# Attention values taken two or three query blocks at a time in the early part of a fused attention and MLP kernel

## The chip, the cores and the metric

The kernel runs on one core of one Trainium2 chip. The metric is device time of one execution in microseconds (us). All matrix work is in 32-bit floating point. The engines are named as in the profile: PE (matrix products; PEld is its weight loading), DVE (vector), ACT (activation and copies), POOL (general elementwise) and SP (issues transfers).

## The reference

```python
# q, k, v: (8, 8, 576, 64); tau = 0.02; w_in: (512, 2048); w_out: (2048, 512)
scores = matmul(q, k^T) / 8
scores = where(scores >= max(scores) - tau, scores, -1e9)
attn   = exp(scores - max(scores));  attn = attn / (sum(attn) + 1e-9)
o      = matmul(attn, v)                       # (8, 8, 576, 64)
x      = o.transpose(0, 2, 1, 3).reshape(4608, 512)
out    = square(maximum(x @ w_in, 0)) @ w_out  # (4608, 512)
```

## The kernel before

Attention and the MLP run together as one stream on PE. Attention is cut into *visits* (one pair of heads of one batch, or half of it) and *steps* (one block of 128 queries of a visit; block 4 holds the last 64 queries of both heads of the pair). Steps are numbered s0, s1, and so on, in order of time:

- Visits 0 to 3 hold blocks 0 and 1 of the four head pairs of the first batch: steps s0 to s7.
- Visits 4 to 7 hold blocks 2, 3 and 4 of the same pairs: s8 to s19.
- Visits 8, 9 and 10 hold all five blocks of a pair of the second batch: s20 to s34.
- From visit 11 on (s35 and later) the weights are turned by DVE and placed by DMA ("by_dma"). The change does not touch these visits.

In a step, in this order: `scores` (L246) multiplies a block of queries by the keys into the PSUM tiles `s0` and `s1` (one for each head of the pair, one buffer each); DVE takes the row maximum (L268); ACT makes threshold and bias (L281, L282) and the exponents (L284); DVE applies the threshold and sums (L296), which also frees the PSUM tiles for the next step's scores; POOL divides (L304, L306). So each step's scores wait for the DVE threshold of the step before.

Two steps later `turn` turns the weights of the block on PE against the identity (L330, for block 4 L336 and L342), in three parts, each with an ACT copy into `wT` (L331, L338, L343). Parts 0 and 1 stand right behind the scores in PE's order, part 2 later in the step. `mix` (L432) multiplies the turned weights by the values `vs` into a PSUM bank, and `put` copies the result on ACT into `xT`, the input of the MLP (L415; the wide copies of the later visits have lines L419 and L426). In visits 0 to 10, before the change, there is one mix for each block, three steps after its scores: 128 columns wide, 64 for block 4. In PE's order it stands between the turn parts 1 and 2, with a quarter of the step's fill ahead of it. Turn parts 0, 1, 2 and the mix take PSUM banks 4 and 5 by turns (while `early()`, that is before s10, part 1 takes bank 6 or 7). One table says when a mix is made, `mixes`, and `complete` says from which step the tokens of an MLP chunk (256 tokens) may be used.

Between these parts PE is *filled* with MLP work, in pieces of some 1.8 us (`fill`, a quarter of the step's amount at each of four places): `mlp_in` (L480, with ACT L490 and POOL L491 behind it) and `mlp_out` (L519) for chunk 0, and seven `product`s (L552) for each later chunk. How many pieces a step gets is counted when the program is written, from constants, by `rate`: until step `out_from` (s34) only the 32 pieces of chunk 0 are spread, from s10 on.

In the same steps the MLP weights are loaded and rounded, 32 pieces in all, one in most steps from s8 to s34 and two in s15, s18 and s22. A piece takes two ACT instructions (L138, L139), two on DVE (L141, L143) and two on POOL (L145, L147), in this order. The second piece of a step has its ACT part behind the exponents and its DVE L141 ahead of the threshold L296. The `mlp_in` pieces of chunk 0 wait for the rounded `w_in_sb` (L147).

The order on every engine is the order in which the program is written; there is no scheduler behind it.

Of the kernel before, what the change touches and what calls it, by code (L numbers as in the profile page):

```python
# [19 lines left out]
def kernel(  # L20
# [10 lines left out]
    nc = tc.nc  # L31
    B, H, S, D = q.shape
    d_model, d_ff = moe_w_in.shape
    n_tokens = out.shape[0]
    P = 128
    HP = H // 2
    NPAIR = B * HP
    NBLK = S // P
    REST = S - NBLK * P
# [32 lines left out]
    wT = const.tile([P, NC9, S + REST], FP32, name="wT")  # L72
# [3 lines left out]
    at = RAW * 2 * WP  # L76
# [115 lines left out]
    def arrived(t):  # L192
        assert all(x[0].tensor.name != t.tensor.name for x in loads)
# [117 lines left out]
    def take(what, among):  # L311
        used[what] += 1
        return bank[among[used[what] % len(among)]]

    def next_bank():

        among = (4, 5, 6, 7) if state["step"] > first_dma + 2 else (6, 7)
        used["bank"] = min([x for x in among if x > used["bank"]] or among)
        return bank[used["bank"]]

    def turn(vis, i, part):

        w = weights[vis, i][0]
        ps = take("mm", (6, 7)) if early() and part == 1 else take("tx", (4, 5))
        ps = ps.rearrange("p (c n) -> p c n", n=P)
        if i < NBLK:
            cols = slice(i * P, (i + 1) * P)
            for n in range(3):
                c = 3 * part + n
                nc.tensor.transpose(ps[:, n, :], w.rearrange("p u k -> p (u k)")[:, c * P:(c + 1) * P], ident)  # L330
            nc.scalar.copy(wT[:, 3 * part:3 * part + 3, cols], ps[:, 0:3, :])  # L331
        elif part < 2:
            rows = slice(part * D, (part + 1) * D)
            for c in range(NBLK):
                at = part * REST + c * P
                nc.tensor.transpose(ps[:, c, 0:D], w[rows, 0, at:at + P], ident[rows, rows])  # L336
            at = part * (NBLK + 1)
            nc.scalar.copy(wT[:, at:at + NBLK, NBLK * P:S], ps[:, :, 0:D])  # L338
        else:

            for rows, keys in ((slice(0, D), slice(S - REST, S)), (slice(D, P), slice(0, REST))):
                nc.tensor.matmul(ps[rows, 0, 0:D], w[rows, 0, keys], ident[rows, rows], start=True, stop=True)  # L342
            nc.scalar.copy(wT[:, NBLK, NBLK * P:S], ps[:, 0, 0:D])  # L343

    blocks = {}

# [53 lines left out]
    def put(n, first, ps, by_32s):  # L400

        b, pr = divmod(visits[n][0], HP)
        count = ps.shape[1]
        lo = (b * S + first) % RING
        assert b * S + first + count - RING <= read_to["x"]

        def to(x0, x1):
            at = (lo + x0) % RING
            return xT[:, pr, at:at + x1 - x0]

        fit = min(RING - lo, count)
        if not by_32s:
            for x0, x1 in ((0, fit), (fit, count)):
                if x0 < x1:
                    nc.scalar.copy(to(x0, x1), ps[:, x0:x1])  # L415
            return
        src = ps.rearrange("p (b u q) -> p b u q", u=2, b=4)
        if fit == count:
            nc.scalar.copy(to(0, count).rearrange("p (u b q) -> p b u q", u=2, b=4), src)  # L419
            return  # L420

        for u in range(2):
            b0 = min(max((fit - u * P) // 32, 0), 4)
            for x0, x1 in ((0, b0), (b0, 4)):
                if x0 < x1:
                    nc.scalar.copy(to(u * P + x0 * 32, u * P + x1 * 32).rearrange("p (b q) -> p b q", q=32),  # L426
                                   src[:, x0:x1, u, :])

    def mix(n, cols):

        def term(ps, u, c, at, rows=slice(0, P), first=False, last=False):
            nc.tensor.matmul(ps[u * D:(u + 1) * D, :], vs[n % 2][rows, u * (NBLK + 1) + c, :],  # L432
                             wT[rows, NBLK if c == NBLK else u * (NBLK + 1) + c, at:at + ps.shape[1]],
                             start=first, stop=last)

        above, below = slice(0, D), slice(D, P)
        arrived(vs[n % 2])
        if not by_dma(n):
            ps = take("tx", (4, 5))[:, 0:cols.stop - cols.start]
            for c in range(NBLK):  # L440
                for u in range(2):
                    term(ps, u, c, cols.start, first=(c == 0))
            for u, rows in enumerate((above, below)):
                term(ps, u, NBLK, cols.start, rows, last=True)
            put(n, cols.start, ps, False)
            return
        n1, n2 = 2 * P + REST, 2 * P
        at = ODD if paired(n) and n % 2 else ONE
        one, two = (next_bank() for x in range(2))
        groups = (one[:, 0:n1], at, (above, below)), (two[:, 0:n2], TWO, (below, above))  # L450
        for c in range(NBLK):
            for ps, x, _ in groups:
                for u in range(2):
                    term(ps, u, c, x, first=(c == 0))

        for ps, x, places in groups:
            for u, rows in enumerate(places):
                term(ps, u, NBLK, x, rows, last=True)
        put(n, 0, one[:, ONE - at:ONE - at + 2 * P], True)
        left = ODD if at == ODD else LEFT - at  # L460
        put(n, NBLK * P, one[:, left:left + REST], False)
        put(n, 2 * P, two[:, 0:n2], True)
# [123 lines left out]
    FIRST = TCH // P  # L586
    visits = [(g_, list(range(FIRST))) for g_ in range(HP)] + [(g_, list(range(FIRST, NBLK + 1))) for g_ in range(HP)]
    visits += [(g_, list(range(NBLK + 1))) for g_ in range(HP, NPAIR)]

    def paired(n):  # L590

        return n >= 3 * HP
# [8 lines left out]
    def by_dma(n):  # L601

        return n >= 3 * HP - 1
# [6 lines left out]
    for s, (n, i) in enumerate(steps):  # L610

        if by_dma(n):
            mixed = {visits[n][1][-1]: (0, 4)}
        else:
            mixed = {x: (x, 3) for x in range(NBLK + 1)}
        if i in mixed:
            first, lag = mixed[i]
            cols = slice(first * P, S if by_dma(n) else min((i + 1) * P, S))
            mixes[s + lag] = (n, cols)
            g_ = visits[n][0]  # L620
            if g_ % HP == HP - 1:
                complete[s + lag] = g_ // HP * S + cols.stop
# [12 lines left out]
    def early():  # L635
        return state["step"] < min(chunk_at)
# [52 lines left out]
    for s, (n, i) in enumerate(steps):  # L689
        if s < HP * FIRST:  # L690
            x = int(n > 0 and i == 0)
        else:
            x = 2 if (n, i) in ((2 * HP - 2, FIRST + 1), (2 * HP - 1, FIRST + 1), (2 * HP, FIRST)) else 1
# [14 lines left out]
    for s, (n, i) in enumerate(steps):  # L708
# [20 lines left out]
        if more:  # L729
            a, b, c, d = (s + 1, s + 5, s + 7, s + 8) if paired(n) else (s + 1, s + 2, s + 4, s + 4)  # L730
# [26 lines left out]
    for s in range(END + 1):  # L757
# [9 lines left out]
        if on:  # L767
            n, i = steps[s]
            at = visits[n][1].index(i)
            last = at == len(visits[n][1]) - 1  # L770
# [15 lines left out]
        if old:  # L786
            turn(*old, 0)
            turn(*old, 1)
# [11 lines left out]
        if s in mixes and not old:  # L800
            mix(*mixes[s])
            for j in chunk_at.get(s, ()):
                add_chunk(j)
        quarter = rate(s) / 4 if s < END else 1e9
        fill(quarter)
        if s in mixes and old:
            mix(*mixes[s])
            for j in chunk_at.get(s, ()):
                add_chunk(j)
        if old:  # L810
            turn(*old, 2)
# [18 lines left out]
        if 0 < s <= NST and by_dma(steps[s - 1][0]):  # L830
            m, x = steps[s - 1]
# [54 lines left out]
```

## Time and profile before

| | |
|---|---|
| median of 3 runs | 1389.96 us (1389.86 to 1391.53) |
| the profiled execution's own time | 1391.53 us |
| its span, first to last instruction | 1389.8 us |
| PE / DVE / ACT / POOL busy, share of the span | 97% / 60% / 32% / 65% |
| mean granted PE clock | 0.995 of full |
| PE busy from 24.0 to 62.8 us (s3 to s9) | 34.59 of 38.80 us |
| PE busy from 62.8 to 146.9 us (s10 to s22) | 76.43 of 84.10 us |
| PE busy from 146.9 to 216.0 us (s23 to s34) | 66.40 of 69.10 us |
| PE busy from 249.0 to 1389.0 us | 1132.04 of 1140.00 us |

The profiled execution is the slowest of the three, 1.57 us above the median. A busy PE is PE with a matmul in flight. In the timeline a row merges instructions of one kind that follow each other; a bracket at its end gives the idle time of its engine ahead of it, and what ended it. A product in 32-bit floating point appears as two rows in the counts of the trace, so a mix of 10 products has x20.

### The profile page before, as it was taken

Reading aid. Unit: us, or ns where it says so; the run is one execution under the profiler, and the core shown is the slowest. Engines: PE = TensorE matmul, PEld = TensorE weight load, DVE = VectorE, ACT = ScalarE, POOL = GpSimd, SP = SyncE. Lnnn points to the kernel's source line nnn. Section 1 sums busy time; section 2 is a strip of 40 time slices with the busy share of each in tenths; the row PEclk is TensorE's granted clock in tenths of the full one; section 3 lists DMA queues with packets and bytes.
Section 4 is the critical chain, followed back from the end, with each engine's and each line's share of the span. In section 5 each row is a group of like instructions: output and inputs, shape, how many; then the busy total and the mean of one; then the engine's idle time right before and its main releaser. Section 6 shows DMA issues by size and latency. Waiting matters only on the chain.

```text
span 1389.8 us, 22678 instructions
## 1 busy us (share of the span) xinstructions
PE 1354.5 (97%) x7576; PEld 1039.6 (75%) x7576; DVE 828.9 (60%) x1866; ACT 439.8 (32%) x1068; POOL 899.3 (65%) x1211
## 2 busy tenths in 40 slices
PE   6898999999999999999999999999999999999998
PEld 5676556777777777787777778777777877788887
DVE  5877675967767676757565757566666665401001
ACT  4776674223232323232223232322222222210110
POOL 3678875668786968686767677676867655422332
PEclk8999999999999999999999999999999999999999
DMA  8763531445545455554445355544445544310000
GB/s 154 157 152 107 143 93 29 88 85 106 115 98 115 97 109 114 105 112 94 92 87 113 76 111 107 112 87 97 93 93 91 118 89 102 64 31 16 0 16 16
DMA packets 407748, 127.95 MB, mean 92 GB/s; under 512 B 390832, under 2 KB 396752, under 8 KB 407632
## 3 DMA queue, kind: packets, MB, share of 16 engines
q1 hardware_dynamic: 385344, 94.57, 36.1%
q0 software_dynamic: 19984, 31.63, 8.4%
q8 instruction: 61, 1.00, 0.3%
q10 hardware_dynamic: 2304, 0.29, 0.2%
q14 instruction: 55, 0.45, 0.1%
HBM read 50.59 MB, written 9.44 MB: 43 GB/s over the span
## 4 chain that ended last, share of the span: by engine, by line
PE 89%; DVE 3%; ACT 3%; POOL 2%; issue 1%; DMA 1%; SPq 0%; DVEq 0%; ACTq 0%; POOLq 0%
PE bank L480 34%; PE bank L552 29%; PE s L246 12%; PE bank L432 11%; PE bank L519 2%; PE bank L330 2%; ACT wT L331 1%; ACT w L284 1%; DVE wo L507 1%; DVE w L296 1%; DVE st L268 1%; POOL g L491 0%; POOL w L306 0%; POOL w_in_sb L147 0%; DVE wo L296 0%
## 5 line engine op out<-in xcount | busy, mean ns | idle before, releaser
L480 PE MATMUL bank<-xT,w_in_sb 128*128 128x256 f32 x2304 | 520.4, 382 | 3.2 <-POOL w_in_sb L147 2.1
L480 PEld LDWEIGHTS bank<-xT,w_in_sb 128*128 128x128 f32 x2304 | 430.8, 190 | 85.8 <-issue 22.2
L268 DVE TENSOR_REDUCE st<-s 128x1 f32<-128x576 f32 x286 | 204.1, 753 | 224.4 <-PE s L246 224.3
L296 DVE SCALAR_TENSOR_TENSOR w<-s,st,w 128x576 f32<-128x576 f32 x269 | 209.2, 815 | 120.6 <-ACT w L284 120.5
L552 PE MATMUL bank<-wo,gsum 128*128 128x256 f32 x1088 | 248.9, 382 | 2.4 <-POOL gsum L470 2.4
L306 POOL TENSOR_SCALAR w<-w,st 128x576 f32<-128x576 f32 x269 | 223.5, 840 | 25.2 <-DVE st L299 19.2
L552 PEld LDWEIGHTS bank<-wo,gsum 128*128 128x128 f32 x1088 | 203.9, 190 | 41.5 <-issue 9.8
L491 POOL TENSOR_TENSOR g<-g 128x512 f32<-128x512 f32 x144 | 152.1, 1057 | 96.4 <-ACT g L490 95.1
L281 ACT ACTIVATE st<-st 128x2 f32<-128x2 f32 (+1 forms) x148 | 30.3, 205 | 566.1 <-DVE st L268 565.4
L552 PE MATMUL bank<-wo,g 128*128 128x256 f32 x816 | 188.3, 382 | 0.0
L284 ACT ACTIVATE w<-s,st 128x576 f32<-128x576 f32 x269 | 183.3, 732 | 0.2 <-ACT st L282 0.2
L370 DVE STREAM_TRANSPOSE turned<-w 128x512 f32<-128x512 f32 (+2 forms) x388 | 168.8, 490 | 18.7 <-DMA wT<-turned 16.7
L246 PE MATMUL s<-kT,qT 64*128 64x288 f32 x1016 | 166.9, 435 | 12.1 <-DVE kT L226 4.9
L304 POOL TENSOR_SCALAR st<-st 128x2 f32<-128x2 f32 (+1 forms) x148 | 32.9, 222 | 221.6 <-DVE w L296 214.4
L552 PEld LDWEIGHTS bank<-wo,g 128*128 128x128 f32 x816 | 153.0, 190 | 30.0 <-issue 8.7
L432 PE MATMUL bank<-wT,vs 128*64 128x128 f32 (+7 forms) x1700 | 167.8, 356 | 5.1 <-ACT wT L331 3.5
L432 PEld LDWEIGHTS bank<-wT,vs 128*64 128x64 f32 (+1 forms) x1700 | 95.5, 136 | 76.8 <-issue 24.6
L490 ACT ACTIVATE g<-bank 128x512 f32<-128x512 f32 x144 | 86.1, 599 | 194.8 <-PE bank L480 194.2
L246 PEld LDWEIGHTS s<-kT,qT 64*128 64x128 f32 x1016 | 94.9, 189 | 69.1 <-issue 49.0
L190 POOL DMA_DIRECT2D vs<-in_v_dram x144 | 90.7, 635 | 0.0
L566 DVE TENSOR_TENSOR gsum<-g 128x512 f32<-128x512 f32 x34 | 23.0, 707 | 110.6 <-PE bank L552 110.6
L145 POOL TENSOR_TENSOR turned<-turned 128x512 f32<-128x512 f32 x32 | 41.1, 1288 | 40.7 <-DVE turned L143 34.9
(80 smaller groups left out, 1006.1 us busy)
## 6 DMA issues: line engine op xcount, KB each, us to landing
wT<-turned SPq DMA_DIRECT2D x800, 72.0 KB, 2.3
out_dram<-osb POOLq DMA_DIRECT2D x34, 256.0 KB, 2.8
wo<-in_moe_w_in_dram SPq DMA_DIRECT2D x16, 512.0 KB, 4.7
wo<-in_moe_w_out_dram SPq DMA_DIRECT2D x16, 512.0 KB, 3.6
ql<-in_q_dram POOLq DMA_DIRECT2D x96, 72.0 KB, 2.7
wT<-turned SPq DMA_DIRECT2D x192, 36.0 KB, 2.3
kl<-in_k_dram POOLq DMA_DIRECT2D x88, 72.0 KB, 3.0
vs<-in_v_dram POOLq DMA_DIRECT2D x48, 128.0 KB, 3.1
```

Source lines behind the costliest of these rows:

```text
L190: (nc.gpsimd if state["step"] > first_dma + 2 else nc.sync).dma_start(out=to, in_=src)
L246: nc.tensor.matmul(sc[u][to, half, 0:HALF], lhsT, keys[rows, half * HALF:(half + 1) * HALF], start=True, stop=True)
L268: nc.vector.tensor_reduce(out=mx[:, u:u + 1], in_=sc[u][:, :, 0:HALF], axis=AX.XY, op=ALU.max)
L284: nc.scalar.activation(out=w[:, u, :].rearrange("p (h k) -> p h k", h=2), in_=sc[u][:, :, 0:HALF], func=AF.Exp, bias=bias[:, u:u + 1], sca ...
L296: nc.vector.scalar_tensor_tensor(out=wu, in0=sc[u][:, :, 0:HALF], scalar=thr[:, u:u + 1], in1=wu, op0=ALU.is_ge, op1=ALU.mult, accum_out=s ...
L306: nc.gpsimd.tensor_scalar(out=w[:, u, :], in0=w[:, u, :], scalar1=z[:, u:u + 1], scalar2=rcp[:, u:u + 1], op0=ALU.add, op1=ALU.mult)
L370: nc.vector.transpose(wb[:, at:at + k1 - k0, i % 2, :], w[:, u, k0 * 32:k1 * 32].rearrange("p (k q) -> p k q", q=32))
L432: nc.tensor.matmul(ps[u * D:(u + 1) * D, :], vs[n % 2][rows, u * (NBLK + 1) + c, :], wT[rows, NBLK if c == NBLK else u * (NBLK + 1) + c, a ...
L480: nc.tensor.matmul(h[:, x % 2, :], w_in_sb[:, c, f * P:(f + 1) * P], xT[:, c, at:at + TCH], start=(c == 0), stop=(c == NMC - 1))
L490: nc.scalar.activation(out=to, in_=h, func=AF.Relu)
L491: nc.gpsimd.tensor_tensor(out=to, in0=to, in1=to, op=ALU.mult)
L552: nc.tensor.matmul(to, left[:, f, :], wo[:, slot, f, :], start=(f == 0), stop=(f == HF - 1))
```

## The change

Visits 0 to 10 are mixed in two goes instead of block by block: blocks 0 and 1 together (256 columns), three steps after block 1's scores, and blocks 2, 3 and 4 together (320 columns), three steps after block 4's scores. So 35 mixes (28 of 128 columns, 7 of 64) become 14 (7 of 256 columns, 7 of 320), with 10 products each as before, and 35 copies by `put` become 14. The mixes that stay keep their places in PE's order; 21 are gone: those of s3, s5, s7, s9, of s11, s12, s14, s15, s17, s18, s20, s21, and of s23, s25, s26, s28, s30, s31, s33, s35, s36.

Since the turned weights of a half visit now wait longer for their mix, half visits put theirs in two places of `wT` by turns (`column`): columns 0 to 319 for even visits, 320 to 639 for odd ones. Whole visits keep theirs.

```diff
+    def column(vis, i):
+
+        first = visits[vis][1][0]
+        return i * P if len(visits[vis][1]) > NBLK else vis % 2 * (S + REST) // 2 + (i - first) * P
+
     def turn(vis, i, part):
 ...
         if i < NBLK:
-            cols = slice(i * P, (i + 1) * P)
+            cols = slice(column(vis, i), column(vis, i) + P)
 ...
-            nc.scalar.copy(wT[:, at:at + NBLK, NBLK * P:S], ps[:, :, 0:D])
+            x = column(vis, i)
+            nc.scalar.copy(wT[:, at:at + NBLK, x:x + D], ps[:, :, 0:D])
 ...
-            nc.scalar.copy(wT[:, NBLK, NBLK * P:S], ps[:, 0, 0:D])
+            x = column(vis, i)
+            nc.scalar.copy(wT[:, NBLK, x:x + D], ps[:, 0, 0:D])
 ...
         if not by_dma(n):
             ps = take("tx", (4, 5))[:, 0:cols.stop - cols.start]
+            at = column(n, cols.start // P)
             for c in range(NBLK):
                 for u in range(2):
-                    term(ps, u, c, cols.start, first=(c == 0))
+                    term(ps, u, c, at, first=(c == 0))
             for u, rows in enumerate((above, below)):
-                term(ps, u, NBLK, cols.start, rows, last=True)
+                term(ps, u, NBLK, at, rows, last=True)
 ...
         if by_dma(n):
             mixed = {visits[n][1][-1]: (0, 4)}
         else:
-            mixed = {x: (x, 3) for x in range(NBLK + 1)}
+
+            mixed = {FIRST - 1: (0, 3), NBLK: (FIRST, 3)}
```

In the built program the instructions on DVE, POOL and SP stand in the same order as before, row by row. On PE and ACT the 21 mixes and their copies are missing and 14 are wider; nothing else has moved.

## The prediction

> **What bounds the kernel now.** First the page: busy shares, the span in slices and the PE clock.
>
> ```profile
> PE 1354.5 (97%) x7576; PEld 1039.6 (75%) x7576; DVE 828.9 (60%) x1866; ACT 439.8 (32%) x1068; POOL 899.3 (65%) x1211
> ...
> PE   6898999999999999999999999999999999999998
> ```
>
> PE is the bound, but not everywhere. From 249 us on it idles 8 of 1140 us, and the change leaves that part alone: whatever s3 to s37 gain or lose shifts it as a whole. The early part, 24 to 249 us, has idle PE: 4.2 us in s3 to s9, 7.7 in s10 to s22, 2.7 in s23 to s34. So I went through the timeline there step by step, asking of each step whether PE's work or something else lets the next scores start.
>
> A step before s10, in PE's timeline (s4, then the scores of s5):
>
> ```profile
> 33.57 1.46 PE L432 MATMUL bank<-wT,vs 128*64 128x128 f32 x20
> 34.96 0.55 PE L330 MATMUL bank<-ident,w 128*128 128x128 f32 x3
> 36.15 1.94 PE L246 MATMUL s<-kT,qT 64*128 64x288 f32 x8 [0.65 <-DVE wo L296]
> ```
>
> The mix takes 1.39 us (33.57 to 34.96); then PE waits 0.65 us for the threshold. The loop scores, maximum, exponents, threshold, scores sets these steps (5.26 us each), not PE. Later, with pieces of MLP work in the steps, PE sets most, but not all. All engines in s15, a step with two weight pieces:
>
> ```profile
> 95.72 1.35 ACT L284 ACTIVATE w<-s,st 128x576 f32<-128x576 f32 x2
> ...
> 96.96 0.66 ACT L138 ACTIVATE turned<-wo 128x512 f32<-128x512 f32 x1
> 97.72 0.43 DVE L141 TENSOR_SCALAR turned<-turned 128x512 uint32<-128x512 uint32 x1 [1.15 <-ACT turned L138]
> 98.06 0.81 DVE L296 SCALAR_TENSOR_TENSOR w<-s,st,w 128x576 f32<-128x576 f32 x1
> ...
> 99.03 1.21 PE L246 MATMUL s<-kT,qmid 128*128 128x288 f32 x4 [0.90 <-ACT wT L343]
> ```
>
> The second piece's L138 and L141 stand ahead of the threshold; PE starts 0.23 us after the first L296 has ended (98.80), whatever the bracket names. PE in s17:
>
> ```profile
> 107.68 0.70 PE L480 MATMUL bank<-xT,w_in_sb 128*128 128x256 f32 x2 [0.50 <-POOL w_in_sb L147]
> 108.91 0.70 PE L480 MATMUL bank<-xT,w_in_sb 128*128 128x256 f32 x2 [0.53 <-POOL w_in_sb L147]
> ```
>
> Here POOL's rounding is late; its chain hangs on s16, not on PE.
>
> **The price of a mix.** The narrow ones are in the trace: 1.39 us for 128 columns and, from the next rows, 0.88 (82.31 to 83.19) for 64.
>
> ```profile
> 82.31 0.95 PE L432 MATMUL bank<-wT,vs 128*64 128x64 f32 x20 [0.24 <-ACT wT L331]
> 83.19 0.55 PE L330 MATMUL bank<-ident,w 128*128 128x128 f32 x3
> ```
>
> The wide ones occur only in later visits, where one mix does a 256- and a 320-column group:
>
> ```profile
> 291.92 4.79 PE L432 MATMUL bank<-wT,vs 128*64 128x320 f32 x40
> 296.63 1.99 PE L480 MATMUL bank<-xT,w_in_sb 128*128 128x256 f32 x8
> ```
>
> 4.71 us over 576 columns, shared by columns: 2.10 for 256 and 2.62 for 320. The upper bound goes on from the narrow rows, 0.51 us for each 64 columns: 2.41 and 2.92. I take the lower, since those rows have the widths themselves. PE work before: 28 x 1.39 + 7 x 0.88 = 45.1 us; after: 7 x (2.10 + 2.62) = 33.0. Freed 12.1 us (7.8 by the upper bound). A step that loses its mix gives PE 1.39 us; one that keeps it pays 0.71 (256 for 128) or 1.74 (320 for 64).
>
> **Step by step.** Freed PE time counts only down to the time at which the threshold or POOL lets the next scores start; an added cost counts in full wherever PE has no idle time. Ready times are those at which L296 ends, plus the 0.22 us seen above.
>
> - s3 to s9: the removals free nothing (PE idles already; s3 ends on the threshold too, 30.66). The 256s in s4 and s8 put 0.71 against 0.65 idle, +0.09 each with rounding; s6 has 0.95 idle: 0. Sum +0.2.
> - s10, s11: s10 pays 0.71, has 0.33 idle. But s11's maximum starts at 69.43, behind L143 of DVE, not behind the scores, so s10's loss is absorbed and s11 gives a little: -0.15.
> - s12 (-1.39; two fill pieces, PE sets it) and s13 (+1.74): +0.35.
> - s14 -1.39. s15: nothing, the threshold sets it. s16 +1.74. s17 -1.39, and the two POOL waits of 0.50 and 0.53 go as well: L147 is ready at 107.6 and 108.85, while s16 has made PE 1.74 later. Sum -2.07.
> - s18: nothing (1.22 idle ahead of s19, second piece again). s19 +1.74, s20 -1.39 and two waits of 0.54 and 0.54, s21 -0.3 (threshold). Sum -1.0.
> - s22 to s24: POOL is behind by a step there (busy without a gap from 147.07 to 163.9), and L139, queued on ACT behind L147 and ahead of the turn copies, holds s24's mix until 155.24. Counted from the start of s22 (139.26): that mix still starts at +16.0, then 2.10 + 0.38 + two pieces of 3.53 give s25 at +22.06, against 21.28. The 1.39 of s23 is lost in that wait: +0.78.
> - s25 -0.8, s26 -0.3 (thresholds ready 165.06 and 170.93 against scores at 166.41 and 171.77; the second head's half comes 0.8 later and takes part of it), s27 +1.74: +0.64.
> - s28 -0.7 (threshold 183.46, scores 184.41), s29 +0.71: 0.
> - s30 -0.4, s31 -0.1, s32 and s33 together +0.82 (s33 falls to its loop, 4.55 from 5.66), s34 0.71 less 0.33 idle: +0.7.
> - s35 -1.36, s36 -1.39 (three pieces and more, PE sets them), s37 +1.74: -1.0.
>
> Sum -1.5 us. Of 12.1 us freed, over ten vanish: the mixes spread the work evenly, and in two goes the full steps grow fuller while the emptied ones hit the loop.
>
> Costed at nothing: `put`. 28 x 0.265 + 7 x 0.217 us of copies go, 7 x 0.383 and 7 x about 0.43 (between the 256-wide 0.383 and the 384-wide 0.482 of L331) come: ACT gains 3.2 us. The copies stand behind the exponents; queued behind them are the turn copy and the weight pieces, read a step later. If they were on the loop, that is 3.2 us more gain at most, and a loss of 0.2 at each 320. The turn part 2 now reuses the bank of part 0 and waits for its copy, as the removed mix did (0.24 us, kept in the times above). Chunk 1 joins the queue a step later (s22), when only chunk 0's pieces are dealt: 0. The values of visit 2 and 3 overwrite those of visit 0 and 1 after a mix that ends 0.71 later; SP's queue has q and k loads behind, but issues at 38.08 what s7 and s8 read: 0, or 0.7 once for each if SP had no slack.
>
> **The clock.** Windows of 2 us; columns: PE, PEld, DVE, ACT, POOL busy, then the clock:
>
> ```profile
> 14.00:16.00 2.00, 0.00 (x0) 0.00 (x0) 1.86 (x7) 1.72 (x5) 0.20 (x1) 0.99 0.79 205
> 16.00:18.00 2.00, 0.24 (x2) 0.27 (x4) 1.99 (x4) 0.85 (x2) 1.66 (x3) 0.50 1.01 389
> ...
> 26.00:28.00 2.00, 2.00 (x8) 1.24 (x7) 1.74 (x3) 0.17 (x1) 1.83 (x4) 0.50 0.73 118
> 28.00:30.00 2.00, 2.00 (x21) 1.50 (x19) 1.18 (x3) 1.84 (x6) 2.00 (x2) 0.59 0.94 203
> ```
>
> PE stops at 12.85, and at 16 the clock is halved; it comes back at about 29.6, after PE has run without a gap since 23.97. The mix of s3 lies in that run (28.36 to 30.35). Without it PE runs from 23.97 to about 28.95 and then idles until 30.86. If the clock then stays halved into s4, s4 costs: scores 3.0 for 1.9, turns 1.5 for 0.9, half the mix at half speed: together about +2.3 us. In s5, s7 and s9 PE now idles 1.4 + 0.65 = 2.0 us at a stretch; the largest idle stretch at which the clock stayed up is 0.95 (s6), the one that lost it was over 3. I take 2.0 as harmless, being nearer the first.
>
> [...]
>
> **The rivals.**
>
> *Little gain* (42%): the sum above, clock back in s3: 1389.96 - 1.5 = about 1388.5. The profiled execution is 1.57 us above the median; the difference is applied to the median. Its own range is 1386 to 1391.
>
> *Clock late once* (20%): -1.5 + 2.3: 1390.8. For it: the run of s3 is cut from over 10 us to 5. Against: 5 us is as long as PE needed before.
>
> *More of the freed time comes through* (20%): in s11, s21, s25, s26, s28, s30 and s31 the loop keeps back 7 x 1.39 - 2.75 = 7.0 us. Part of what sets it is DVE's L141, 0.42 us when alone but 1.0 to 1.5 in several of these steps while POOL works; with POOL further ahead after the long steps it may shrink. Half of the 7.0 gives -5: 1385; all of it -8.5: 1381.5.
>
> *Slower: the clock falls in the emptied early steps* (18%). If an idle stretch of 2.0 us is enough, each of s5, s7, s9 hands a halved clock to s6, s8, s10. The price of a halved clock is in s3: 6.92 us against 5.26 for the same work, 1.66, and up to 2.3 with a 256-column mix. With s4's that is about +8: 1396.5. It decides once idle stretches between 0.95 and 3.1 us are enough. The upper price of the wide mixes (+0.3 in ten steps set by PE) makes the same side, +1.5 net.
>
> That the change doesn't do what it says I exclude: in the built program 35 mixes are 14 wide ones.
>
> **How the numbers follow.** 1388.5 is the likeliest. The range holds little gain, late clock with the upper mix price (1390.8 + 3.0 = about 1394), and the third case to half and somewhat over (1383); left out are its far end and most of the slower one. A measurement of this kernel can tell about 0.2%, 2.8 us: below 1387.2 or above 1392.7. Faster: 20% from the third case and 13% from the first, whose step limits are each good to a few tenths. Slower: 18%, 5% from the second, 2% from the first. The same: 42%.
>
> **What would show it.** Right: scores still 5.26 us apart from s5 to s9 with 2 us of PE idle in s5, s7, s9; the POOL waits of s17 and s20 gone; s15 and s18 as long as before (6.34 and 6.66 us); wide mixes of 2.1 and 2.6 us; from s38 on the same spacing as before. Wrong: a PE clock under 1 after 33 us, steps without a mix shorter than 4.5 us with two heads, or a lasting difference after 250 us.

## The result, and the profile after

| | before | after |
|---|---|---|
| median | 1389.95 us (4 runs, 1389.86 to 1391.53) | 1399.72 us (4 runs, 1398.81 to 1400.27) |
| ratio | | 1.0067, 95% interval 1.0049 to 1.0084 |
| span of the profiled execution | 1389.8 us | 1398.5 us |
| mean granted PE clock in it | 0.995 | 0.984 |
| the same, 30 to 73 us | 1.00 | 0.74 |

The kernel became 0.7% slower, 9.8 us. The forecast was 1388.5 with a range of 1383 to 1394; the rival that had the clock falling in the emptied early steps, 1396.5, named the cause.

From the page of the changed kernel: the busy time and instruction count of each engine, the PE clock in 40 slices, and the group of `mlp_in` products (now L488).

```profile
PE 1357.4 (97%) x7156; PEld 1027.4 (73%) x7156; DVE 826.4 (59%) x1866; ACT 440.1 (31%) x1047; POOL 898.9 (64%) x1211
...
PEclk7799999999999999999999999999999999999999
...
L488 PE MATMUL bank<-xT,w_in_sb 128*128 128x256 f32 x2304 | 519.3, 382 | 1.1 <-ACT osb L533 1.1
```

PE has 420 rows fewer and yet 2.9 us more busy time: part of its work ran at half speed. The clock is down in the first two slices (0 to 70 us); before it was down in the first alone. (It also falls for 3.4 us each at 107.1 and 127.6 us, too short to show in a slice.) The POOL waits of `mlp_in` are gone, as forecast. Now the windows of 2 us, with columns as in the prediction (PE busy first, PE clock third from the end):

```profile
38.00:40.00 2.00, 1.79 (x15) 1.17 (x11) 1.32 (x2) 0.83 (x2) 1.83 (x3) 1.00 0.88 174
40.00:42.00 2.00, 0.00 (x0) 0.00 (x0) 2.00 (x4) 1.90 (x6) 2.00 (x3) 1.00 0.98 270
42.00:44.00 2.00, 1.69 (x6) 1.57 (x7) 1.22 (x6) 1.29 (x3) 0.79 (x3) 0.57 0.57 101
44.00:46.00 2.00, 2.00 (x9) 1.10 (x6) 1.40 (x2) 0.00 (x0) 1.12 (x2) 0.50 0.53 84
46.00:48.00 2.00, 2.00 (x10) 1.14 (x10) 0.43 (x2) 1.67 (x5) 0.00 (x0) 0.50 0.77 125
48.00:50.00 2.00, 2.00 (x14) 1.05 (x12) 1.71 (x5) 0.86 (x2) 0.00 (x0) 0.72 0.89 201
```

PE stands still from 39.79 to 42.31, in the emptied s5, and the clock is halved just as s6 begins. PE's timeline of the same stretch:

```profile
38.59 1.20 PE L335 MATMUL bank<-ident,w 128*128 128x128 f32 x9
42.31 2.99 PE L246 MATMUL s<-kT,qT 64*128 64x288 f32 x8 [2.52 <-DVE w L296]
45.23 1.54 PE L335 MATMUL bank<-ident,wo 128*128 128x128 f32 x6
46.70 3.70 PE L439 MATMUL bank<-wT,vs 128*64 128x256 f32 x20
50.33 0.55 PE L335 MATMUL bank<-ident,wo 128*128 128x128 f32 x3
```

Nine turns in a row (parts 0, 1, 2), then 2.52 us of nothing, then scores in 2.99, turns in 1.54 and the mix in 3.63 us (46.70 to 50.33). With the clock up, the same scores and turns took 1.94 and 0.87 us before (s6, 41.41 to 44.16), and a mix of this width takes 2.46 (first run below). The starts of the steps say what this costs, in us from one step's scores to the next one's:

| step | s4 | s5 | s6 | s7 | s8 | s9 | s10 | sum |
|---|---|---|---|---|---|---|---|---|
| before | 5.26 | 5.26 | 5.57 | 5.26 | 5.26 | 5.32 | 4.59 | 36.52 |
| after | 8.25 | 4.90 | 8.50 | 4.89 | 8.63 | 4.83 | 6.38 | 46.38 |

Those seven steps lose 9.9 us. In s6, s8 and s10 the clock had just fallen, at 42.28, 55.9 and 69.6 us. In s4 it had not come back yet: it was halved from 15.0 to 35.5 us, where before it was halved from 16.0 to 29.6. From s11 to s41 the two profiled executions part by 0.6 us more, and before s4 the one of before was 1.7 us later by its own start: 9.9 + 0.6 - 1.7 is the 8.7 by which the spans differ.

### The profile page after: what moved, and what is told of

Its sections match the earlier page's. It is cut to its first block, busy times and chain, and to the rows that moved or that the text cites. A ratio compares the mean times of both kernels' runs of the same rounds, so it can differ in the third digit from the quotient of the medians.

```text
span 1398.5 us, 21810 instructions
## 1 busy us (share of the span) xinstructions
PE 1357.4 (97%) x7156; PEld 1027.4 (73%) x7156; DVE 826.4 (59%) x1866; ACT 440.1 (31%) x1047; POOL 898.9 (64%) x1211
## 4 chain that ended last, share of the span: by engine, by line
PE 93%; DVE 3%; ACT 2%; POOL 1%; issue 1%; DMA 0%; SPq 0%; DVEq 0%; ACTq 0%; POOLq 0%
PE bank L488 35%; PE bank L560 29%; PE s L246 13%; PE bank L439 12%; PE bank L335 2%; DVE st L268 1%; PE bank L527 1%; DVE w L296 1%; ACT w L284 1%; POOL kl L190 0%; POOL g L499 0%; DMA wo<-in_k_dram 0%; ACT wT L336 0%; POOL w L306 0%; DVE wo L296 0%
## 5 line engine op out<-in xcount | busy, mean ns | idle before, releaser
L488 PE MATMUL bank<-xT,w_in_sb 128*128 128x256 f32 x2304 | 519.3, 382 | 1.1 <-ACT osb L533 1.1
L488 PEld LDWEIGHTS bank<-xT,w_in_sb 128*128 128x128 f32 x2304 | 431.1, 190 | 82.7 <-issue 22.7
L246 PE MATMUL s<-kT,qT 64*128 64x288 f32 x1016 | 169.8, 440 | 17.5 <-DVE w L296 7.8
L439 PE MATMUL bank<-wT,vs 128*64 128x256 f32 (+3 forms) x1280 | 164.5, 424 | 1.0 <-ACT wT L336 1.0
L439 PEld LDWEIGHTS bank<-wT,vs 128*64 128x64 f32 (+1 forms) x1280 | 80.5, 140 | 78.9 <-issue 29.8
```

The source lines that it names most:

```text
L246: nc.tensor.matmul(sc[u][to, half, 0:HALF], lhsT, keys[rows, half * HALF:(half + 1) * HALF], start=True, stop=True)
L488: nc.tensor.matmul(h[:, x % 2, :], w_in_sb[:, c, f * P:(f + 1) * P], xT[:, c, at:at + TCH], start=(c == 0), stop=(c == NMC - 1))
```

## The experiments

Each kernel was compared with the kernel before on the same chip.

**The removed mixes made again, for nothing.**

```diff
+        if n < HP and i == 0:
+            again[s + 3] = (n, slice(0, P))
 ...
+        if s in again:
+            mix(*again[s], keep=False)      # without put()
```

> The changed kernel, but in s3, s5, s7 and s9 the removed 128-column mix is made again and its result is left unused (no copy); all 14 wide mixes stay. So PE has the work of before in the emptied early steps, and everything else is as changed. Clock theory (PE idles over 2 us in these steps, the clock is halved, and the next step runs at half speed): the clock stays up from about 30 us, scores come every 5.3 to 5.7 us from s4 to s9, and the time falls from 1399.7 by 8 to 9 to 1390.5 to 1392. Theory of the uneven steps (the wide mixes are dear and the loop is hit, whatever the clock): the extra work gives nothing back, 1398 to 1401.

Measured: 1390.55 us (10 runs, 1389.46 to 1391.35), ratio 1.0004, interval 0.9994 to 1.0013. More work, 9 us less time. PE's timeline, s5 and s6:

```profile
36.12 1.46 PE L439 MATMUL bank<-wT,vs 128*64 128x128 f32 x20
37.51 0.55 PE L335 MATMUL bank<-ident,w 128*128 128x128 f32 x3
38.70 1.95 PE L246 MATMUL s<-kT,qT 64*128 64x288 f32 x8 [0.64 <-DVE w L296]
40.58 0.87 PE L335 MATMUL bank<-ident,wo 128*128 128x128 f32 x6
41.38 2.53 PE L439 MATMUL bank<-wT,vs 128*64 128x256 f32 x20
```

PE idles 0.64 us as before, the clock is 1.00 from 28 us through all early steps, and the 256-column mix takes 2.46 us. (It falls later, at 95.9 and 116.4 us for 3.4 us each, behind the idle stretches of s15 and s18, whose mixes are not made again.) The wide mixes themselves cost hardly anything in these steps: s4 takes 5.38 us, s6 5.62. Steps s5 and s7 take 4.90, less than the 5.3 expected.

**One third of the change at a time.** In `mixed`, the two goes for some visits and block by block for the others:

```diff
-            mixed = {FIRST - 1: (0, 3), NBLK: (FIRST, 3)}
+            mixed = {FIRST - 1: (0, 3), NBLK: (FIRST, 3)} if n < HP else {x: (x, 3) for x in range(NBLK + 1)}
```

and the same with `HP <= n < 2 * HP`, and with `n >= 2 * HP`.

Visits 0 to 3 alone: 

> Only visits 0 to 3 are mixed in one go of 256 columns; visits 4 to 10 block by block as before. Clock theory: nearly the whole loss, 1397.5 to 1400, with the clock halved in s6, s8 and s10. Uneven steps: a wide mix costs at most 1.06 against 0.65 idle four times, so 1390 to 1392.

Visits 4 to 7 alone: 

> Only visits 4 to 7 are mixed in one go of 320 columns. Clock theory: the clock falls only behind the long idle stretches of s15 and s18 (2.3 us in the changed kernel), two 320-column mixes at half speed, about +2 and otherwise -1: 1389.5 to 1392. Uneven steps alone, with 2.99 us for the wide mix: 1389 to 1391, the clock at 1 throughout after 30 us.

Visits 8 to 10 alone: 

> Only visits 8 to 10 are mixed in two goes (256 and 320 columns). No idle stretch over 1 us follows, so both theories have the clock at 1 after 30 us. In the changed kernel s23 to s38 took 1.6 us longer than before, and 2.0 came back by s41, so 1388.5 to 1391.5; the prediction's sum for this part (s23 to s37 some 0.4 gained) gives 1389.5.

| in two goes | median | ratio, interval | granted clock, all runs |
|---|---|---|---|
| visits 0 to 3 | 1398.48 us | 1.0063, 1.0048 to 1.0078 | 0.985 to 0.988 |
| visits 4 to 7 | 1391.17 us | 1.0011, 1.0001 to 1.0020 | 0.992 to 0.994 |
| visits 8 to 10 | 1391.13 us | 1.0006, 0.9996 to 1.0015 | 0.994 to 0.996 |

The early visits alone have 8.6 of the 9.8 us, with the clock down as in the full change. The other two thirds each lose about 1 us, at the edge of what can be told. For visits 4 to 7 the clock theory was only half right: it expected the clock to fall behind s15 and s18, as in the changed kernel, but in this profile it stayed up (granted 1.00 from 64 to 150 us) although PE idled 2.25 us ahead of s16 and 3.22 us ahead of s19. The profiled execution is the fastest of the ten; the others have 0.992 or 0.993, which would fit a fall or two there, but no trace shows it.

**Five idle turns in each emptied step.** Products with the identity into a free PSUM bank, which nothing reads:

```diff
+    def busy(times):
+        ...
+        to = ... bank[4 + (used["tx"] + 1) % 2]
+        for x in range(times):
+            nc.tensor.transpose(to[:, 384:512], ident, ident)
 ...
+            busy({3: 5, 5: 5, 7: 5, 9: 5}.get(s, 0))     # end of the step
```

> The changed kernel with 5 turns of the identity (0.65 us) in s3, s5, s7 and s9, so that PE idles about 1.85 us at a stretch instead of 2.5. It asks from which idle stretch the clock falls. If 1.85 us is still enough: 1397 to 1400 as changed; if it is not: 1390.5 to 1391.5; in between, if it falls in some steps only (2.3 to 2.8 us for each fall).

Measured: median 1391.82 us, ratio 1.0026 (1.0009 to 1.0043), but the ten runs lie from 1389.42 to 1399.11: six below 1392.5 with a granted clock of 0.993, four from 1395 to 1399 with 0.986 to 0.989. The profiled execution is one of the four:

```profile
38.07 0.77 PE L284 MATMUL bank<-ident 128*128 128x128 f32 x5
40.67 3.00 PE L246 MATMUL s<-kT,qT 64*128 64x288 f32 x8 [1.84 <-DVE w L304]
43.59 1.54 PE L343 MATMUL bank<-ident,wo 128*128 128x128 f32 x6
45.06 3.75 PE L446 MATMUL bank<-wT,vs 128*64 128x256 f32 x20
```

So the same program, with PE idle 1.84 us at a stretch in this profile, loses the clock here in s6, s8 and s10 and, by time and granted clock, keeps it in six other executions. The stretch alone does not decide: in this profile the clock also fell at 30.50 us, behind only 1.03 us of idle time ahead of s4.

**Eight idle turns.** The same with 8 in place of 5.

> The changed kernel with 8 turns of the identity in s3, s5, s7 and s9: PE idles some 1.4 us at a stretch. With 5 turns (1.85 us) the clock fell in some executions only. Clock theory: at 1.4 us it stays up in all of them, 1389.5 to 1391.5, all runs within 2 us, granted clock 0.99; if the edge is lower, some runs lie above 1394.

Measured: 1391.11 us, ratio 1.0012 (1.0003 to 1.0022), ten runs from 1388.77 to 1393.41, granted clock 0.991 to 0.995. None comes near the 1395 to 1399 of the run with five, but four lie at 1393.0 to 1393.4 with 0.991, and no trace shows where those lost their clock. PE idles 1.2 us per emptied step, and in the profile the clock is 1.00 from 30 to 80 us. The spread was 4.6 us rather than the 2 expected. In the profile the clock fell once more, at 115.97 us behind 3.21 us of idle time ahead of s19, since s15 and s18 have no idle work; behind the idle stretch ahead of s16 it stayed up (the mean clock from 80 to 150 us is 0.98, no more than one such fall).

**Idle work at the start of the kernel before**, where its clock was halved from 16 to 29.6 us: `busy({0: 20, 2: 8})`, in s0 into s0's own PSUM tile.

> The kernel before, with idle PE work at the start: 20 turns of the identity, never read, behind s0's threshold (into s0's own PSUM tile) and 8 at the end of s2 (into the free one of banks 4 and 5). Clock theory: in the kernel before the clock is halved from 16 to 29.6 us, and s2 and s3 take 6.2 and 6.9 us against 5.3 in s4 to s9; if PE is kept busy they take 5.3 to 5.5, and the time falls by 1.7 to 2.5 to 1387.5 to 1388.3. If the clock falls in spite of it, or loads set s2 and s3, 1389.5 to 1391.

Measured: 1389.04 us, ratio 0.9996 (0.9986 to 1.0005): a miss. The clock came back at 19.2 instead of 29.6, and s2 and s3 took 5.03 and 5.26 us; but the 20 turns, at half speed, ran until 18.56 and held up s2's scores, which start at 18.61; they start at 17.76 in the profile of before and at 16.0 to 16.2 in most others.

**Idle work in all emptied or waiting steps of the changed kernel**: `busy({0: 20, 2: 8, 3: 12, 5: 12, 7: 12, 9: 12, 15: 12, 18: 12})`.

> The changed kernel with idle PE work wherever PE would idle long: 20 and 8 turns of the identity in s0 and s2, 12 each (1.6 us) in s3, s5, s7, s9, s15 and s18, never read. Clock theory: the clock at 1 throughout; 1390.5 (run with the removed mixes made again) less 1.7 to 2.5 at the start and less 0 to 1 at s16 and s19: 1387 to 1389, no better than the kernel before with the same work at the start. If the uneven steps cost on their own, 1390 to 1392.

Measured: 1388.53 us, ratio 0.9993 (0.9984 to 1.0003). Granted clocks of 0.996 to 0.999. With the clock held the changed kernel is not slower than the one before.

**The same two with 13 turns in s0 instead of 20.**

The changed kernel: 

> The changed kernel with the idle PE work of the run before last (all emptied or waiting steps), but 13 turns instead of 20 in s0, since the 20 ran 1 us into s2's scores. Clock theory: s2 starts at 16 to 16.5 us instead of 17.15, and the gain at the start is kept: 0.5 to 1 below 1388.5, so 1387.5 to 1388.2, some 1.5 to 2 below the kernel before. If 13 turns don't bring the clock back early, 1388.5 to 1390.

The kernel before: 

> The kernel before with 13 turns of the identity in s0 and 8 in s2. Clock theory: 1387.8 to 1388.8, and within 0.7 of the changed kernel with idle work in all emptied steps, since the clock is the only large thing that parts the two; uneven steps: the changed one is 1 to 2 slower than this one.

Measured: 1388.07 us for the changed kernel, ratio 0.9988 (0.9979 to 0.9997), and 1388.55 for the one before, 0.9989 (0.9980 to 0.9998). Both are a little faster than the kernel before, by 1.9 and 1.4 us; the expected 1387.5 to 1388.2 and 1387.8 to 1388.8 hold, though the eleven runs of the changed kernel lie from 1386.15 to 1391.72. What parts them, 0.5 us, is inside the intervals: with the clock held in both, taking the values in two goes is worth nothing that can be told.

## Why the prediction was wrong

- **The step that failed** is in the part on the clock: "I take 2.0 as harmless, being nearer the first." Twice wrong. The stretch was 2.5 us, not 2.0: behind a long step the two heads' scores run in one go, 1.25 us where they took 1.94 before, so PE is done earlier still. And it was not harmless: the clock fell behind it in s5, s7 and s9, 1.84 us lost it in the profile with five idle turns, and the removed mixes made again gave back 9 us. Choosing by the nearer of 0.95 and 3.1 had no ground; the case deserved far more than 18%. Nor does the length of a stretch settle it: 1.03 us lost the clock once and 3.22 us kept it once, as shown below.
- **A second rival came true with it.** "Clock late once" was priced by itself; in the changed kernel s4 ran at half speed too, because the clock came back only at 35.5 us. So the loss is one late return (s4) and three falls (s6, s8, s10).
- **The price of a fall** was set at 2.3 us at most. Measured: +3.0, +2.9 and +3.4 in s4, s6, s8 and +1.8 in s10, less 0.4 to 0.5 in each of s5, s7, s9, which got shorter. Against the run with the removed mixes made again, whose mixes are as wide, half speed costs 2.9 to 3.0 in s4, s6 and s8: the scores go from 1.94 to 2.99 us and the mix from 2.45 to between 3.4 and 3.8.
- **PE was not idle all the time ahead of a fall.** From the mean clocks of the 2 us windows the clock of the changed kernel changes at 42.28, 49.12, 55.9, 62.8 and 69.6 us, 6.8 apart; the shortest time between two changes in that profile is 3.41 us. Two of its stretches of that length, each ending with a fall:

```profile
38.87:42.28 3.41, 0.92 (x9) 0.69 (x8) 3.41 (x7) 3.00 (x8) 3.08 (x4) 1.00 0.90 235
103.72:107.13 3.41, 1.26 (x6) 1.03 (x7) 2.62 (x9) 3.35 (x9) 0.98 (x1) 1.00 0.33 95
```

  PE was busy for 27% of the first and 37% of the second, and the clock fell behind both. The fall of before, at 15.97 us, came behind 0.29 us of work in 3.41 (12.56 to 15.97). From the first record to 155 us the clock falls seven times in the profiles of before and after, each time behind 3.41 us with PE busy for 0.00 to 1.26 us. It stayed up in the profile of before behind 97.89 to 101.30 us with PE busy for 2.23 us and behind 118.37 to 121.78 us with 2.06.
- **At one idle length the clock fell in one profile and stayed up in another.** With visits 4 to 7 alone PE idled 3.22 us ahead of s19 and the clock stayed up; with eight idle turns it idled 3.21 us in the same place and the clock fell. First the scores of s19 and two stretches of 3.41 us with visits 4 to 7 alone, over which the idle time is spread (PE busy for 2.02 and 1.58 us), then the same with eight turns, where the first stretch holds nearly all of it (PE busy for 0.45 us) and ends with the fall:

```profile
117.44 1.21 PE L246 MATMUL s<-kT,qmid 128*128 128x288 f32 x4 [3.22 <-ACT turned L138]
112.20:115.62 3.42, 2.02 (x12) 1.44 (x8) 1.62 (x3) 2.87 (x7) 3.23 (x5) 1.00 0.35 131
115.62:119.03 3.41, 1.58 (x9) 1.36 (x10) 3.34 (x10) 2.23 (x7) 0.80 (x2) 1.00 0.53 162
...
116.22 2.26 PE L246 MATMUL s<-kT,qmid 128*128 128x288 f32 x4 [3.21 <-ACT turned L138]
112.56:115.97 3.41, 0.45 (x3) 0.05 (x1) 2.12 (x2) 3.35 (x8) 2.50 (x3) 1.00 0.23 38
115.97:119.39 3.42, 3.17 (x10) 2.49 (x10) 2.70 (x10) 0.93 (x3) 1.72 (x2) 0.50 0.80 256
```

  The falls do not come at one place in the program: in the changed kernel at 107.14 us, 1.27 us behind the start of the scores of s16, and with the removed mixes made again at 95.9 us, 0.7 us behind it. Whether such a difference parts the two groups of runs with five turns is not shown, since only one of those ten runs has a trace. Nor does the busy time of PE settle it: with five turns the clock fell at 30.50 us behind 2.38 us of work in 3.41 (27.09 to 30.50), more than the 2.06 us behind which it stayed up in the profile of before.
- **The price of a wide mix** was mis-sized: 2.10 and 2.62 us, the lower bounds, were taken. PE's timeline of the changed kernel:

```profile
183.30 3.06 PE L439 MATMUL bank<-wT,vs 128*64 128x320 f32 x20
186.29 0.55 PE L335 MATMUL bank<-ident,wo 128*128 128x128 f32 x3
...
195.34 2.53 PE L439 MATMUL bank<-wT,vs 128*64 128x256 f32 x20 [0.24 <-ACT wT L336]
197.79 0.55 PE L335 MATMUL bank<-ident,w 128*128 128x128 f32 x3
```

  2.45 and 2.99 us, at the upper bounds (2.41 and 2.92). With 0.88 and 1.39 for 64 and 128 columns that makes 0.53 us for each 64 columns and 0.35 once for each mix. By these prices the change frees 45.1 - 7 x (2.45 + 2.99) = 7.0 us of PE work, not 12.1. The rows of the later visits were the wrong neighbours, though they had the widths: 4.71 us for 576 columns is no more than 9 x 0.53, so no fixed part shows there. Why it does not, and what it consists of, stays open.
- **The step walk** was right in kind. The POOL waits of s17 and s20 are gone; s15 and s18 take 6.46 us each, against 6.34 and 6.66, though their mix is gone; steps with a 320-column mix and full PE pay for it (s13 +2.1, s37 +2.1), emptied ones with fill gain what PE had (s14 -1.5, s35 -1.5, s36 -1.2). s16 and s19 took 3.4 us more, not 1.74, since the clock fell there too. Its sum, -1.5 us, can be set against the two kernels with the clock held: -0.5 us, with an uncertainty of more than 1. The third with visits 8 to 10 alone, whose profile has the clock at 1.00 from 30 us on, came out 1.2 us slower at the median, with an interval from 0.6 us gained to 2.1 lost; so whether the walk's gain exists is open. That the freed time nearly vanishes between full and emptied steps holds.
- **The rival "more of the freed time comes through"** found no support: with the removed mixes made again or idle turns in their place, no kernel's median came below 1388.

## What to carry to other kernels

Work that is taken off PE is not only time saved: when the trace shows that its clock falls behind idle time, count the idle time that is left, step by step, and ask what the next step costs at half speed. Look at the busy time of PE over a few microseconds and not only at the longest idle stretch: here 1.03 us lost the clock once and 3.22 us kept it once, and the seven falls in the profiles of before and after up to 155 us came behind 3.41 us with PE busy for at most 1.26 us. Expect executions of one program to differ: those with five idle turns took 1389.42 to 1399.11 us. A few idle products in the kernel tell more than the argument about which known stretch is nearer. Gathering the work of short steps into every second step saves the fixed part of each mix (0.35 us here) and hands it back where the steps hit another chain; here it also took away the steady work that had kept the clock up.

## What the runs showed of the hardware

- The clock was halved behind PE idle stretches of 2.44 to 2.52 us every time in s5, s7 and s9 of the changed kernel, and of 1.76 to 1.84 us in those of the profile with five idle turns. Ahead of s16 it fell behind 2.26 us in the changed kernel and behind 2.25 with the removed mixes made again, and stayed up behind 2.25 with visits 4 to 7 alone; ahead of s19 it fell behind 3.21 us with eight idle turns and stayed up behind 3.22 with visits 4 to 7 alone; and with five idle turns it fell once behind 1.03 us.
- In the profiles of before and after, up to 155 us, its changes lie 3.41 us or a whole multiple of it apart (13.65 us from 15.97 to 29.62 in before; 3.41, 6.83, 17.07, 20.48 and 34.13 us in after). The seven falls came behind 3.41 us with PE busy for 0.00 to 1.26 us; with five idle turns it fell once behind 2.38 us; in the profile of before it stayed up behind 2.06 us.
- 3.41 us with PE busy did not always bring it back: 42.29 to 45.70 (3.39 of 3.41 us busy) and 55.94 to 59.35 us (all of it) in the changed kernel did not, the 3.41 us after each did; 69.59 to 73.01 us (all of it) in the changed kernel and, with the removed mixes made again, 17.39 to 20.80 (3.12 of 3.41 us) did.
- The clock listed ahead of the first recorded change is not evidence: in the profile of before, s0's scores took 2.30 us at a listed clock of 1.00, as long as s2's at a listed 0.50; in the run with visits 0 to 3 alone they took 1.25.
